# A fused attention, feed-forward and expert kernel: startup steps, the last output weights' tile, one PSUM bank and the tile of the results are rearranged

## The chip, the cores and the metric

The kernel runs on one core of a Trainium2 chip. The metric is the device time of one execution in microseconds (us). Before the change it was 966.34 us, the median of three runs (966.10, 966.34 and 966.62).

## The reference

Three stages work on 3072 tokens of 512 features; all inputs and outputs are float32.

```python
# 1. attention: 4 x 8 heads, 768 positions, head size 64; each chunk of 32 queries sees
#    8 memory keys, 16 keys to the left, its own 32 and 8 to the right (64 in all)
scores = scale * np.matmul(q_c, k_full.transpose(0, 1, 3, 2))
a = np.exp(scores - np.max(scores, axis=-1, keepdims=True))
a = a / (np.sum(a, axis=-1, keepdims=True) + 1e-09)
out[:, :, c_start:c_end] = np.matmul(a, v_full)
# 2. feed-forward, 512 -> 2048 -> 512
r = np.maximum(x @ w_in, 0.0)
x = (r * r) @ w_out
# 3. one of 8 experts per token (the largest gate logit), 512 -> 1024 -> 512
h = np.maximum(x[mask] @ w1[e], 0.0)
out[mask] = gate_w[mask, None] * eom[mask, e, None] * (h @ w2[e])
```

## The kernel before

The tokens are cut into 12 blocks of 256. A `Duo` is the attention of one block, in two units of 128 tokens (`u0`, `u1`). Its steps have names that the profile's rows carry: `scores_mm` multiplies queries with keys on TensorE (tile pss, L161), `scores_max` and `scores_sub` take the row maximum off on VectorE (mx L190, e L195), `scores_exp` is the exponential on ScalarE (L211), `norm` sums and inverts the rows (sm L217, rs L221) and from duo 2 on also scales e itself (L223), `transpose_a` turns e on TensorE (psa, L234) and copies it back on ScalarE (L244), `av` multiplies with the values (psx, L259 or, in the first two duos, L161), and `transpose_x` turns the result into the pieces xhi (L299) and xlo (L303). The four big tiles pss, psa, psx and pst of all duos follow each other in one PSUM buffer, `ps_a`.

A `Block` is the feed-forward of 256 tokens. Products are made of two pieces per operand, hi and lo: `mm1` is 12 products into ph (L410; for two blocks at once L389), `relu` makes r, g, gh on ScalarE (L421, L429, L433) and gl on VectorE (L435), `mm2` is six products into py (L446 to L448). The weights w_in and w_out come as eight tiles each, i0, o0, i1, ... o7, and each is turned into its pieces by five steps: exponent on ScalarE (L327), shift (L332) and two ORs (L339, L343) on VectorE, hi on ScalarE (L352), lo on VectorE (L357). `wo` and `wi` in the rows are these pieces, `ws_o` and `ws_i` the tiles under conversion.

The gate follows block by block (`gate_transpose`, `gate_logits`, `gate_choose`, `gate_rank`). `gate_rank` counts each token's place in its expert's list with two small products into psr (L528, L529), in a buffer of `ps_h`, a ring of two banks that the ph tiles use too. Then come eight experts' `Pair`s of 256 gathered tokens, and single slots of 128. A pair's tiles end in p (ph0p to ph7p are pair products of the first layer, L734; gl0p L745). `Pair.scale` writes the weighted result to o (L698), from where GpSimd scatters it (L704).

The order is written out by hand at the start (L1014 to L1117) and by a table from position n = 4 on: `todo[n]` holds the steps that are issued at position n of the sequence of first-layer products, sorted by `turn`. `bits` gives the position of each weight tile's ORs (its hi and lo follow one position later), `plan_duo` those of a duo's steps. An engine takes its instructions in the order in which they are issued. At the start `keep_busy(n)` issues n dummy products of `ones` (spin, L1011), each 512 columns wide; `hold` (a small GpSimd copy into the tile that a load will fill) delays a load until a given value exists.

Of the kernel before, what the change touches and what calls it, by code (L numbers as in the profile page):

```python
# [8 lines left out]
F32 = mybir.dt.float32  # L9
# [8 lines left out]
P = 128  # L18
NT = 3072
D = 512  # L20
# [4 lines left out]
NB = NT // BLK  # L25
TPB = BLK // P
# [30 lines left out]
def chunk_attention_relu2_moe_top1_kernel(ctx: ExitStack, tc, qk, vv, qt, kv, w_in, w_out, wg, wexp, consts, out):  # L57
    nc = tc.nc
# [5 lines left out]
    ap_ = ctx.enter_context(tc.tile_pool(name="ap", bufs=2))  # L64
# [257 lines left out]
    def split_w_exp(kind, g, halves=None):  # L322
        t = raw[kind, g]
        if (kind, g) not in converted:
            converted[kind, g] = tp.tile([P, 1024], F32, tag="ws", name=f"ws_{kind}{g}", bufs=2)
        for s in slices(halves):
            nc.scalar.activation(converted[kind, g][:, s], t[:, s, 1].bitcast(F32), ACTF.Abs, scale=2.0 ** -111)  # L327

    def split_w_shift(kind, g, halves=None):
        for s in slices(halves):  # L330
            li = converted[kind, g][:, s].bitcast(I32)
            nc.vector.tensor_scalar(li, li, 3, None, op0=ALU.logical_shift_left)  # L332

    def split_w_or(kind, g, halves=None, steps=(0, 1)):
        t = raw[kind, g]
        for s in slices(halves):
            li = converted[kind, g][:, s].bitcast(I32)
            if 0 in steps:
                nc.vector.scalar_tensor_tensor(  # L339
                    li, t[:, s, 0], 29, li, op0=ALU.logical_shift_right, op1=ALU.bitwise_or  # L340
                )
            if 1 in steps:
                nc.vector.scalar_tensor_tensor(  # L343
                    li, t[:, s, 1], -0x80000000, li, op0=ALU.bitwise_and, op1=ALU.bitwise_or
                )

    def split_w_hi(kind, g, halves=None):
        if (kind, g) not in wh:
            w = wpool.tile([P, 2, 1024], F32R, tag=f"{kind}{g}", name=f"w{kind}{g}")
            wh[kind, g], wl[kind, g] = w[:, 0], w[:, 1]  # L350
        for s in slices(halves):
            nc.scalar.copy(wh[kind, g][:, s], converted[kind, g][:, s])  # L352

    def split_w_lo(kind, g, halves=None):
        for s in slices(halves):
            h, lf = wh[kind, g][:, s], converted[kind, g][:, s]
            nc.vector.tensor_tensor(wl[kind, g][:, s], lf, h.bitcast(F32), op=ALU.subtract)  # L357
# [11 lines left out]
    class Block:  # L369
# [152 lines left out]

        def gate_rank(self):
            b = self.b
            ps = ps_h.tile([P, D], F32, tag="h", name=f"psr{b}")
            n = TPB * NE
            ohf = self.oh.rearrange("p t e -> p (t e)")
            nc.tensor.matmul(ps[:, 0:n], lhsT=before, rhs=ohf, start=True, stop=True)  # L528
            nc.tensor.matmul(ps[:, n : 2 * n], lhsT=ones, rhs=ohf, start=True, stop=True)  # L529
            pb = rp.tile([P, TPB, NE], F32, tag="pb", name=f"pb{b}")  # L530
            pos = rp.tile([P, TPB], F32, tag="pos", name=f"pos{b}")
            idx = rp.tile([P, TPB], I32, tag="idx", name=f"idx{b}", bufs=2)
            for t in range(TPB):
                nc.vector.tensor_tensor(pb[:, t], ps[:, t * NE : (t + 1) * NE], base[:, 0:NE], op=ALU.add)
                nc.vector.tensor_tensor(base[:, 0:NE], base[:, 0:NE], ps[:, n + t * NE : n + (t + 1) * NE], op=ALU.add)
            nc.vector.tensor_tensor(pb, pb, self.oh, op=ALU.mult)
            nc.vector.tensor_reduce(out=pos, in_=pb, axis=AX.X, op=ALU.add)
            nc.vector.tensor_copy(idx, pos)  # L538
            for t in range(TPB):
                nc.gpsimd.indirect_dma_start(  # L540
                    out=listd,
                    out_offset=bass.IndirectOffsetOnAxis(ap=idx[:, t : t + 1].bitcast(U32), axis=0),
                    in_=ent[:, b * TPB + t, :],
                    in_offset=None,
                )
# [89 lines left out]
    class Entry:  # L635
# [50 lines left out]
        def scale(self, t, po, shared=False):  # L686
            c = self.col + t
            if self.tiles == 1:
                o = qp.tile([P, D], F32, tag="q", name=f"o{c}")
            else:  # L690
                if t == 0:
                    self.o = ap_.tile([P, TPB, D], F32, tag="e", name=f"o{c}", bufs=1)
                o = self.o[:, t]
            self.y[t] = o
            weight = slots[:, c, 1:2].bitcast(F32)
            on_act = 0 if self.tiles > 1 else D // 2 if shared else D
            if on_act < D:
                nc.vector.tensor_scalar(o[:, on_act:], po[:, on_act:], weight, None, op0=ALU.mult)  # L698
            if on_act > 0:
                nc.scalar.activation(o[:, :on_act], po[:, :on_act], ACTF.Copy, scale=weight)  # L700
# [160 lines left out]
    def plan_duo(b, s, m, t, v, last=None):  # L861
        d = duos[b]
        plan(s, d.scores)
        plan(m, d.norm)
        plan(t, d.transpose_a)
        plan(v, d.av)
        if last is None:
            plan(v, d.transpose_x_copy)
        else:
            ahead[last] = d.transpose_x_copy  # L870
        if b + 1 < NB:
            plan(s + 1, duos[b + 1].load_q, 0)
            plan(s + 1, duos[b + 1].load_q, 1)
        if 2 < b < NB - 1:
            plan(v + 1, duos[b + 1].load_kv, 1)
        if b < NB - 2:
            plan(v + 2, duos[b + 2].load_kv, 0)
# [5 lines left out]
        plan(c, bl.gate_choose)  # L883
        plan(r, bl.gate_rank)

    bits = dict(zip(range(3, 16), (2, 4, 6, 8, 10, 12, 14, 15, 17, 18, 20, 21, 23)))
    for m, n in bits.items():
        if m > 4:
            plan(bits[m - 1], split_w_exp, *tiles[m])
# [13 lines left out]
    plan(bits[15] + 1, duos[3].load_kv, 1)  # L903
    plan(23, lambda: prepare())
    n = at[2, 0]
    plan_duo(2, n - 7, n - 6, n - 4, n - 3)
    plan_duo(3, n + 1, n + 2, n + 5, n + 6)
    plan_gate(0, n + 7, n + 9, n + 15, n + 18)
    plan_duo(4, n + 11, n + 13, n + 15, n + 17)
# [2 lines left out]
    for g in range(2, GROUPED - 1):  # L912
        n = at[2 * g, 0]
# [74 lines left out]
    with tc.manual_schedule():  # L988
# [6 lines left out]
        def hold(tile_, until):  # L995
            nc.gpsimd.tensor_copy(tile_[0:1, 0:1], until)
# [9 lines left out]

        spin = ps_h.tile([P, 4, P], F32, tag="h", name="spin")

        def keep_busy(n):
            for _ in range(n):  # L1010
                nc.tensor.matmul(spin, lhsT=ones, rhs=ones.unsqueeze(1).to_broadcast([P, 4, P]), start=True, stop=True)  # L1011

        u0, u1, other = (0,), (1,), (ps_y, "y")
        keep_busy(12)  # L1014
        d0.scores_mm(u0)
        keep_busy(4)
        d0.scores_max(u0)
        i0t = load_w(*i0, issue=False)
        hold(i0t[:, 1024:].bitcast(F32), d0.mx[u0][0:1, 0, 0:1])
# [7 lines left out]
        d0.scores_exp(u0)  # L1027
        d0.transpose_a_mm(u0)
        d0.transpose_a_copy(u0)
        keep_busy(3)  # L1030
        d0.scores_max(u1)
        d0.scores_sub(u1)
        d0.scores_exp(u1)
# [1 line left out]
        d0.norm(u0)  # L1035
        d0.av_mm(u0)
        d0.av_scale(u0)
        split_w_shift(*i0, a)
        split_w_or(*i0, a, steps=(0,))
        d0.transpose_a_mm(u1, *other)  # L1040
# [3 lines left out]
        split_w_exp(*i0, b)  # L1044
        keep_busy(2)
        d0.av_mm(u1, *other)
        d0.transpose_x_lo(u0)
        d0.norm(u1)
        i1t = load_w(*i1, issue=False)
        hold(i1t.bitcast(F32), d0.r[u1][0:1, 0, 0:1])  # L1050
        load_w(*i1)
        nc.sync.dma_start(cst[:, P:], consts[:, P:])
        d0.av_scale(u1)
        keep_busy(5)
        split_w_or(*i0, a, steps=(1,))
        d0.transpose_x_mm(u1, *other)
        split_w_shift(*i0, b)
        split_w_hi(*i0, a)
        d0.transpose_x_hi(u1)
        split_w_or(*i0, b, steps=(0,))  # L1060
        split_w_lo(*i0, a)
        d0.transpose_x_lo(u1)
        split_w_or(*i0, b, steps=(1,))
        d1.scores_mm()
        keep_busy(2)
        b0.mm1_products(0)
        split_w_hi(*i0, b)
        load_w(*o1)
        d1.scores_max()
        split_w_lo(*i0, b)  # L1070
        split_w_exp(*o0)
        keep_busy(3)
        d1.scores_sub()
        b0.relu(0)
        b0.mm1_products(1)
        d1.scores_exp()
        split_w_shift(*o0)
        split_w_or(*o0, steps=(0,))
        keep_busy(3)
        d1.transpose_a_mm()  # L1080
        d1.norm()
        split_w_or(*o0, steps=(1,))
        load_w(*i2)
        b0.relu(1)
        d1.transpose_a_copy()
        keep_busy(3)
        d1.av_mm()
        split_w_exp(*i1)
        split_w_hi(*o0)
        d1.av_scale()  # L1090
        split_w_lo(*o0)
        keep_busy(5)
        d1.transpose_x_mm()
        split_w_shift(*i1)
        d1.transpose_x_hi()
        b0.mm2(0)
        d1.transpose_x_lo()
        split_w_exp(*o1)
        b0.mm2(1)
        split_w_or(*i1)  # L1100
        load_w(*o2)
        b1.mm1_products(0)
        split_w_shift(*o1)
        b1.relu(0)
        split_w_hi(*i1)
        b1.mm1_products(1)
        split_w_lo(*i1)
        b1.mm2(0)
        split_w_or(*o1)
        b1.relu(1)  # L1110
        split_w_exp(*i2)
        split_w_hi(*o1)
        split_w_shift(*i2)
# [167 lines left out]
```

## Time and profile before

| what | value |
|---|---|
| median of three runs | 966.34 us |
| the profiled execution | 967.47 us, of it the span 965.5 us |
| TensorE (PE) busy | 945.5 us, 98% of the span |
| VectorE (DVE) busy | 600.1 us, 62% |
| ScalarE (ACT) busy | 453.2 us, 47% |
| GpSimd (POOL) busy | 98.6 us, 10% |
| granted TensorE clock, mean | 0.997 of full |

PE is the engine that carries the program, so the time is its busy time plus its waits plus what a lower clock costs it. A row of the timeline gives start, duration, engine, line, operation, written and read tiles, and in square brackets how long the engine was idle before it and whom it waited for. "issue" means that it waited for nothing that the profile shows.

### The profile page before, as it was taken

The numbers are of one execution on the slowest core, as the hardware profiler recorded it, in microseconds if no ns is written. First come the engines' busy times: TensorE is split into PE (matmuls) and PEld (weight loads), VectorE is DVE, ScalarE is ACT, GpSimd is POOL, SyncE is SP. The second block draws the span as 40 slices with busy tenths as digits, with TensorE's granted clock in tenths as the row PEclk, the third lists the DMA queues.
The fourth block names the chain that finished last, engine by engine and source line by source line (L and its number), as shares of the span: only waits on it lengthen the run. The fifth ranks groups of instructions, "written<-read, shape, count | busy, mean of one in ns | idle before, by whom it ended". The sixth has DMA issues, their size and how long they took to land. (4 is left out here: it accounts for less than half of the span.)

```text
span 965.5 us, 19444 instructions
## 1 busy us (share of the span) xinstructions
PE 945.5 (98%) x7862; PEld 792.1 (82%) x7862; DVE 600.1 (62%) x1125; ACT 453.2 (47%) x816; POOL 98.6 (10%) x93
## 2 busy tenths in 40 slices
PE   7999899999999999999999999999999999999996
PEld 4787789888888888888888888888899999888885
DVE  6999553554445345534553454668776666799995
ACT  4787433323233233332322333545455445688885
POOL 0100000000000000000000011012232212122221
PEclk9999999999999999999999999999999999999999
DMA  9466423223120212021100106360876656553631
GB/s 367 155 223 234 150 87 99 76 24 103 39 76 23 76 67 76 23 75 54 51 1 2 45 1 246 134 240 15 325 309 221 236 209 244 191 188 131 218 124 42
DMA packets 30991, 125.51 MB, mean 130 GB/s; under 512 B 8559, under 2 KB 9071, under 8 KB 21554
## 3 DMA queue, kind: packets, MB, share of 16 engines
q1 hardware_dynamic: 25650, 110.30, 31.9%
q0 software_dynamic: 5248, 13.92, 4.1%
q8 instruction: 64, 1.05, 0.5%
q14 instruction: 29, 0.24, 0.1%
HBM read 138.65 MB, written 13.61 MB: 158 GB/s over the span
## 5 line engine op out<-in xcount | busy, mean ns | idle before, releaser
L389 PE MATMUL ph<-xhi,wi 128*128 128x512 f32 x688 | 212.6, 390 | 0.3 <-DVE wi L357 0.3
L421 ACT ACTIVATE r<-ph 128x256 f32<-128x256 f32 x192 | 72.2, 376 | 234.5 <-PE ph L389 199.0
L431 DVE TENSOR_TENSOR g<-r 128x256 f32<-128x256 f32 x160 | 67.4, 422 | 183.6 <-ACT r L421 183.6
L446 PE MATMUL py<-wo,gh 128*128 128x512 f32 x384 | 156.4, 407 | 0.8 <-ACT gh L433 0.8
L389 PEld LDWEIGHTS ph<-xhi,wi 128*128 128x128 f32 x688 | 129.1, 188 | 28.4 <-DVE wi L357 1.2
L448 PE MATMUL py<-wo,gl 128*128 128x512 f32 x384 | 150.4, 392 | 0.0
L447 PE MATMUL py<-wo,gh 128*128 128x512 f32 x384 | 150.4, 392 | 0.0
L389 PE MATMUL ph<-xlo,wi 128*128 128x512 f32 x344 | 133.9, 389 | 0.0
L683 DVE TENSOR_TENSOR x<-raw,x 128x1024 fp32r<-128x1024 f32 x88 | 103.2, 1222 | 7.0 <-ACT x L682 5.4
L435 DVE TENSOR_TENSOR gl<-g,gh 128x256 fp32r<-128x256 f32 x192 | 81.4, 425 | 31.0 <-ACT gh L433 9.8
L683 DVE TENSOR_TENSOR p<-raw,p 128x1024 fp32r<-128x1024 f32 x64 | 78.2, 1222 | 23.1 <-ACT p L682 23.1
L682 ACT CAST x<-raw 128x1024 fp32r<-128x1024 f32 x88 | 87.3, 1056 | 0.0
L446 PEld LDWEIGHTS py<-wo,gh 128*128 128x128 f32 x384 | 72.3, 188 | 17.3 <-issue 2.0
L448 PEld LDWEIGHTS py<-wo,gl 128*128 128x128 f32 x384 | 72.2, 188 | 16.2 <-DVE gl L435 0.6
L433 ACT ACTIVATE gh<-r 128x256 fp32r<-128x256 f32 x192 | 79.9, 416 | 10.4 <-PE py L447 2.3
L447 PEld LDWEIGHTS py<-wo,gh 128*128 128x128 f32 x384 | 72.4, 189 | 12.5
L540 POOL DMA_INDIRECT listd<-ent,idx x24 | 25.5, 1061 | 555.1 <-DVE idx L538 336.9
L389 PEld LDWEIGHTS ph<-xlo,wi 128*128 128x128 f32 x344 | 64.6, 188 | 13.5
L682 ACT CAST p<-raw 128x1024 fp32r<-128x1024 f32 x64 | 66.6, 1041 | 1.2 <-DMA raw<-in_wexp 1.2
L834 PE MATMUL po<-x,ht 128*128 128x512 f32 x264 | 65.4, 397 | 0.6 <-DVE ht L824 0.6
L704 POOL DMA_INDIRECT out<-o,slots x27 | 37.5, 1390 | 208.6 <-ACT o L700 91.4
L834 PEld LDWEIGHTS po<-x,ht 128*128 128x128 f32 x264 | 48.1, 188 | 10.2 <-DVE ht L824 1.0
(229 smaller groups left out, 1455.7 us busy)
## 6 DMA issues: line engine op xcount, KB each, us to landing
raw<-in_wexp SPq DMA_DIRECT2D x82, 1024.0 KB
kv<-in_kv SPq DMA_DIRECT2D x19, 880.0 KB
raw_o<-in_w_out SPq DMA_DIRECT2D x8, 1024.0 KB
raw_i<-in_w_in SPq DMA_DIRECT2D x7, 1024.0 KB
ydram<-y SPq DMA_DIRECT2D x24, 256.0 KB
q<-in_qt SPq DMA_DIRECT2D x20, 256.0 KB
qk<-in_qk SPq DMA_DIRECT2D x4, 624.0 KB
v<-in_vv SPq DMA_DIRECT2D x2, 1024.0 KB
```

The lines of the kernel that those rows point to most:

```text
L389: nc.tensor.matmul(ph.rearrange("p (s c) -> p s c", s=2), lhsT=w_in_part(w, f, k), rhs=x[:, s, k, :], start=(n == 0), stop=(n == 11),)
L421: nc.scalar.activation(self.r, self.ph, ACTF.Relu, scale=WSCALE)
L431: nc.vector.tensor_tensor(g, r, r, op=ALU.mult)
L433: nc.scalar.activation(gh, r, ACTF.Square)
L435: nc.vector.tensor_tensor(gl, g, gh.bitcast(F32), op=ALU.subtract)
L446: nc.tensor.matmul(self.y[t], lhsT=gh[:, s], rhs=w_out_part(wh, f), start=(f == 0), stop=False)
L447: nc.tensor.matmul(self.y[t], lhsT=gh[:, s], rhs=w_out_part(wl, f), start=False, stop=False)
L448: nc.tensor.matmul(self.y[t], lhsT=gl[:, s], rhs=w_out_part(wh, f), start=False, stop=(f == NF - 1))
L682: nc.scalar.copy(w[:, 0], t)
L683: nc.vector.tensor_tensor(w[:, 1], t, w[:, 0].bitcast(F32), op=ALU.subtract)
L704: nc.gpsimd.indirect_dma_start(out=out, out_offset=bass.IndirectOffsetOnAxis(ap=slots[:, c, 0:1].bitcast(U32), axis=0), in_=self.y[t], in_ ...
L834: nc.tensor.matmul(self.po, lhsT=self.ht[:, part, f, :], rhs=w[:, wp, j * D : j * D + D], start=(f == 0 and part == 0 and wp == 0), stop=( ...
```

## The change

It has five parts. (1) For the last two blocks `gate_rank` takes its bank from `ps_a` instead of the ring `ps_h`. (2) `Pair.scale` takes a tile for each half from the ring t2 (four buffers) instead of both halves in the one buffer of tag e. (3) Tile 15, the last output weights o7, has its ORs at position 26 instead of 23, hi and lo at 27 instead of 24, and with them duo 3's load of keys at 27 instead of 24. (4) Duo 2's `norm` is issued at position 25, with its scores, instead of 26. (5) The start is written in another order: duo 1's scores, maximum and the rest come ahead of the ORs of the second half of i0, block 1's first-layer products ahead of block 0's second layer, and the dummy products are other ones: 36 of 128 columns instead of 12 of 512, 6 of 256 instead of 4 of 512, 10 of 128 instead of 3 of 512, and later ones partly left out.

```diff
         def gate_rank(self):
             b = self.b
-            ps = ps_h.tile([P, D], F32, tag="h", name=f"psr{b}")
+            if b < NB - 2:
+                ps = ps_h.tile([P, D], F32, tag="h", name=f"psr{b}")
+            else:
+                ps = ps_a.tile([P, TPB, D], F32, tag="a", name=f"psr{b}")[:, 0]
...
             else:
-                if t == 0:
-                    self.o = ap_.tile([P, TPB, D], F32, tag="e", name=f"o{c}", bufs=1)
-                o = self.o[:, t]
+                o = tp.tile([P, D], F32, tag="t2", name=f"o{c}")
...
-    bits = dict(zip(range(3, 16), (2, 4, 6, 8, 10, 12, 14, 15, 17, 18, 20, 21, 23)))
+    bits = dict(zip(range(3, 16), (2, 4, 6, 8, 10, 12, 14, 15, 17, 18, 20, 21, 26)))
...
-    plan_duo(2, n - 7, n - 6, n - 4, n - 3)
+    plan_duo(2, n - 7, n - 7, n - 4, n - 3)
...
-        keep_busy(12)
+        keep_busy(36, 1)
         d0.scores_mm(u0)
-        keep_busy(4)
+        keep_busy(6, 2)
...
-        split_w_or(*i0, b, steps=(0,))
         split_w_lo(*i0, a)
         d0.transpose_x_lo(u1)
-        split_w_or(*i0, b, steps=(1,))
+        keep_busy(3)
         d1.scores_mm()
-        keep_busy(2)
         b0.mm1_products(0)
-        split_w_hi(*i0, b)
+        d1.scores_max()
+        d1.scores_sub()
+        split_w_or(*i0, b)
         load_w(*o1)
-        d1.scores_max()
-        split_w_lo(*i0, b)
+        keep_busy(3)
+        d1.scores_exp()
         split_w_exp(*o0)
...
         d1.transpose_a_mm()
         d1.norm()
+        d1.transpose_a_copy()
+        split_w_hi(*i0, b)
+        b0.relu_r(0)
+        split_w_shift(*o0)
+        split_w_lo(*i0, b)
...
+        b1.mm1_products(1)
         b0.mm2(0)
```

The first place is VectorE around the two ORs of o7 and duo 2's maximum; ws_o7 is the tile under conversion, wo7 its lo piece, gl0_12 to gl1_13 are lo pieces of activations of block 0 and 1, and mx2, e2, sm2 and rs2 belong to duo 2. On VectorE before:

```order
L339 SCALAR_TENSOR_TENSOR ws_o7_1142<-raw_o7_1087,ws_o7_1142 128x1024
L343 SCALAR_TENSOR_TENSOR ws_o7_1142<-raw_o7_1087,ws_o7_1142 128x1024
L435 TENSOR_TENSOR gl0_12_1231<-g0_12_1227,gh0_12_1229 128x256
L357 TENSOR_TENSOR wo7_1233<-ws_o7_1142,wo7_1233 128x1024
L435 TENSOR_TENSOR gl1_12_1250<-g1_12_1246,gh1_12_1248 128x256
L190 TENSOR_REDUCE mx2_0_1317<-pss2_0_1252 128x16
L195 TENSOR_TENSOR e2_1319<-pss2_0_1252,mx2_0_1317 128x2x8x64
L207 MEMSET e2_1319 32x8x8
L435 TENSOR_TENSOR gl0_13_1348<-g0_13_1344,gh0_13_1346 128x256
L217 TENSOR_REDUCE sm2_0_1350<-e2_1319 128x16
L218 TENSOR_SCALAR sm2_0_1350<-sm2_0_1350 128x16
L221 RECIPROCAL rs2_0_1353<-sm2_0_1350 128x16
```

On VectorE after the change the same place reads:

```order
L435 TENSOR_TENSOR gl0_12_1253<-g0_12_1249,gh0_12_1251 128x256
L435 TENSOR_TENSOR gl1_12_1267<-g1_12_1263,gh1_12_1265 128x256
L190 TENSOR_REDUCE mx2_0_1334<-pss2_0_1269 128x16
L195 TENSOR_TENSOR e2_1336<-pss2_0_1269,mx2_0_1334 128x2x8x64
L207 MEMSET e2_1336 32x8x8
L217 TENSOR_REDUCE sm2_0_1340<-e2_1336 128x16
L218 TENSOR_SCALAR sm2_0_1340<-sm2_0_1340 128x16
L221 RECIPROCAL rs2_0_1343<-sm2_0_1340 128x16
L223 TENSOR_TENSOR e2_1336<-e2_1336,rs2_0_1343 128x1024
L435 TENSOR_TENSOR gl0_13_1371<-g0_13_1367,gh0_13_1369 128x256
L339 SCALAR_TENSOR_TENSOR ws_o7_1166<-raw_o7_1111,ws_o7_1166 128x1024
L343 SCALAR_TENSOR_TENSOR ws_o7_1166<-raw_o7_1111,ws_o7_1166 128x1024
```

The two ORs stand behind duo 2's last scaling of e (L223) instead of ahead of its maximum, the lo piece wo7 is later still, and the sum (L217) no longer stands behind gl0_13.

The second place is ScalarE from duo 2's exponential to the copy of the turned e. On ScalarE before, from o7's hi piece on:

```order
L352 CAST wo7_1233<-ws_o7_1142 128x1024
L421 ACTIVATE r1_12_1244<-ph0_12_1212 128x256
L429 ACTIVATE g1_12_1246<-r1_12_1244 128x256
L433 ACTIVATE gh1_12_1248<-r1_12_1244 128x256
L211 ACTIVATE e2_1319<-e2_1319 128x1024
L421 ACTIVATE r0_13_1342<-ph0_13_1329 128x256
```

On ScalarE after the change, from the exponential on:

```order
L211 ACTIVATE e2_1336<-e2_1336 128x1024
L421 ACTIVATE r0_13_1365<-ph0_13_1352 128x256
L429 ACTIVATE g0_13_1367<-r0_13_1365 128x256
L433 ACTIVATE gh0_13_1369<-r0_13_1365 128x256
L421 ACTIVATE r1_13_1385<-ph0_13_1352 128x256
L429 ACTIVATE g1_13_1387<-r1_13_1385 128x256
L433 ACTIVATE gh1_13_1389<-r1_13_1385 128x256
L352 CAST wo7_1393<-ws_o7_1166 128x1024
L421 ACTIVATE r0_14_1417<-ph0_14_1404 128x256
L429 ACTIVATE g0_14_1419<-r0_14_1417 128x256
L433 ACTIVATE gh0_14_1421<-r0_14_1417 128x256
L244 COPY e2_1336<-psa2_0_1425 128x1024
```

The hi piece of o7 has gone from ahead of the exponential to a place ahead of three activations of block 0 and of the copy (L244).

The third place is VectorE at the start, around duo 1's maximum; ws_i0 and wi0 are the second half of the first weights (one wi0 and one OR are of the first half), xlo is duo 0's. On VectorE before:

```order
L343 SCALAR_TENSOR_TENSOR ws_i0_236<-raw_i0_123,ws_i0_236 128x512
L332 TENSOR_SCALAR ws_i0_236<-ws_i0_236 128x512
L339 SCALAR_TENSOR_TENSOR ws_i0_236<-raw_i0_123,ws_i0_236 128x512
L357 TENSOR_TENSOR wi0_351<-ws_i0_236,wi0_351 128x512
L303 TENSOR_TENSOR xlo_110<-pst0_1_345,xhi_109 128x4x128
L343 SCALAR_TENSOR_TENSOR ws_i0_236<-raw_i0_123,ws_i0_236 128x512
L190 TENSOR_REDUCE mx1_0_441<-pss1_0_358 128x16
L357 TENSOR_TENSOR wi0_351<-ws_i0_236,wi0_351 128x512
L195 TENSOR_TENSOR e1_449<-pss1_0_358,mx1_0_441 128x2x8x64
```

On VectorE after the change:

```order
L332 TENSOR_SCALAR ws_i0_269<-ws_i0_269 128x512
L357 TENSOR_TENSOR wi0_382<-ws_i0_269,wi0_382 128x512
L303 TENSOR_TENSOR xlo_110<-pst0_1_376,xhi_109 128x4x128
L190 TENSOR_REDUCE mx1_0_468<-pss1_0_390 128x16
L195 TENSOR_TENSOR e1_470<-pss1_0_390,mx1_0_468 128x2x8x64
L339 SCALAR_TENSOR_TENSOR ws_i0_269<-raw_i0_123,ws_i0_269 128x512
L343 SCALAR_TENSOR_TENSOR ws_i0_269<-raw_i0_123,ws_i0_269 128x512
L217 TENSOR_REDUCE sm1_0_491<-e1_470 128x16
L218 TENSOR_SCALAR sm1_0_491<-sm1_0_491 128x16
L221 RECIPROCAL rs1_0_494<-sm1_0_491 128x16
L332 TENSOR_SCALAR ws_o0_480<-ws_o0_480 128x1024
L357 TENSOR_TENSOR wi0_382<-ws_i0_269,wi0_382 128x512
```

The maximum stood behind both ORs of the second half and now stands ahead of them, and that half's lo piece (the last row) comes behind duo 1's sum instead of right behind the maximum.

## Rows read from the trace of the kernel before

**Rows 1.** Page: busy time of the engines, with shares and counts of instructions

```profile
PE 945.5 (98%) x7862; PEld 792.1 (82%) x7862; DVE 600.1 (62%) x1125; ACT 453.2 (47%) x816; POOL 98.6 (10%) x93
```

**Rows 2.** Waits of PE: sum, times, longest, in us

```profile
PE psa L234 <- DVE e L223: 3.2, 1, 3.2
PE pss L161 <- issue: 2.1, 1, 2.1
PE ph2p L734 <- DVE gl2p L745: 1.8, 1, 1.8
...
PE ph1p L734 <- DVE gl0p L745: 0.8, 1, 0.8
```

**Rows 3.** Windows: length, busy us (instructions) by engine, granted clock, DMA

```profile
core 0: us, PE busy (x) PEld busy (x) DVE busy (x) ACT busy (x) POOL busy (x), PEclk, DMA share, GB/s
...
13.00:24.00 11.00, 8.10 (x229) 6.13 (x228) 9.39 (x16) 5.38 (x10) 0.18 (x1) 1.00 1.02 422
...
42.00:108.00 66.00, 65.20 (x406) 52.71 (x405) 60.86 (x73) 49.23 (x93) 0.00 (x0) 1.00 0.67 235
...
112.00:117.00 5.00, 4.96 (x86) 4.06 (x90) 0.99 (x3) 2.13 (x4) 0.00 (x0) 0.66 0.01 3
...
650.00:692.00 42.00, 39.35 (x252) 35.00 (x251) 32.28 (x87) 19.48 (x30) 11.25 (x9) 1.00 0.36 134
```

**Rows 4.** Timeline of PE at the start

```profile
16.34 0.76 PE L161 MATMUL pss<-qk 64*32 64x64 f32 x52
19.17 1.00 PE L161 MATMUL pss<-qk 64*32 64x64 f32 x76 [2.07 <-issue]
```

**Rows 5.** Timeline of DVE at the start

```profile
20.21 1.23 DVE L190 TENSOR_REDUCE mx<-pss 128x16 f32<-128x1024 f32 x1 [0.99 <-PE pss L161]
...
37.41 1.23 DVE L357 TENSOR_TENSOR wi<-ws_i,wi 128x1024 fp32r<-128x1024 f32 x1 [0.51 <-ACT wi L352]
```

**Rows 6.** Timeline of DVE around o7 and duo 2's maximum

```profile
98.65 1.22 DVE L339 SCALAR_TENSOR_TENSOR ws_o<-raw_o,ws_o 128x1024 int32<-128x1024 int32 x1
99.90 1.23 DVE L343 SCALAR_TENSOR_TENSOR ws_o<-raw_o,ws_o 128x1024 int32<-128x1024 int32 x1
...
102.25 1.23 DVE L357 TENSOR_TENSOR wo<-ws_o,wo 128x1024 fp32r<-128x1024 f32 x1 [0.78 <-ACT wo L352]
...
103.72 1.22 DVE L190 TENSOR_REDUCE mx<-pss 128x16 f32<-128x1024 f32 x1
...
108.93 1.21 DVE L217 TENSOR_REDUCE sm<-e 128x16 f32<-128x1024 f32 x1
...
110.67 1.23 DVE L223 TENSOR_TENSOR e<-e,rs 128x1024 f32<-128x1024 f32 x1
```

**Rows 7.** Timeline of ACT in the same stretch

```profile
98.80 0.40 ACT L433 ACTIVATE gh<-r 128x256 fp32r<-128x256 f32 x1
101.16 1.05 ACT L352 CAST wo<-ws_o 128x1024 fp32r<-128x1024 f32 x1 [1.96 <-DVE ws_o L343]
...
106.47 1.06 ACT L211 ACTIVATE e<-e 128x1024 f32<-128x1024 f32 x1 [3.22 <-PE py L448]
...
113.14 1.01 ACT L244 COPY e<-psa 128x1024 f32<-128x1024 f32 x1 [2.54 <-PE psa L234]
```

**Rows 8.** Timeline of PE around duo 2's psa and psx

```profile
112.04 1.06 PE L234 MATMUL psa<-cst,e 128*128 128x128 f32 x8 [3.22 <-DVE e L223]
112.86 0.48 PE L446 MATMUL py<-wo,gh 128*128 128x512 f32 x1
113.18 0.43 PE L447 MATMUL py<-wo,gh 128*128 128x512 f32 x1
...
115.25 0.32 PE L259 MATMUL psx<-e,v 64*64 64x32 f32 x2
...
```

**Rows 9.** Timeline of PE at the next to last rank

```profile
654.92 0.51 PE L734 MATMUL ph1p<-xhi,p 128*128 128x256 f32 x2 [0.82 <-DVE gl0p L745]
```

**Rows 10.** Timeline of DVE at the first pair's results

```profile
690.08 1.41 DVE L698 TENSOR_SCALAR o<-po,slots 128x512 f32<-128x512 f32 x2 [1.31 <-DMA out<-o,slots]
```

More of the change, by code (lines that the diff above doesn't have):

```diff
@@ L1007, in chunk_attention_relu2_moe_top1_kernel, with keep_busy @@
         spin = ps_h.tile([P, 4, P], F32, tag="h", name="spin")
-        def keep_busy(n):
+        def keep_busy(n, k=4):
             for _ in range(n):
-                nc.tensor.matmul(spin, lhsT=ones, rhs=ones.unsqueeze(1).to_broadcast([P, 4, P]), start=True, stop=True)
+                nc.tensor.matmul(
+                    spin[:, :k], lhsT=ones, rhs=ones.unsqueeze(1).to_broadcast([P, k, P]), start=True, stop=True
+                )
         u0, u1, other = (0,), (1,), (ps_y, "y")
-        keep_busy(12)
+        keep_busy(36, 1)
         d0.scores_mm(u0)
-        keep_busy(4)
+        keep_busy(6, 2)
         d0.scores_max(u0)
@@ L1029, in chunk_attention_relu2_moe_top1_kernel @@
         d0.transpose_a_copy(u0)
-        keep_busy(3)
+        keep_busy(10, 1)
         d0.scores_max(u1)
@@ L1037, in chunk_attention_relu2_moe_top1_kernel @@
         d0.av_scale(u0)
+        d0.norm(u1)
         split_w_shift(*i0, a)
@@ L1046, in chunk_attention_relu2_moe_top1_kernel @@
         d0.av_mm(u1, *other)
-        d0.transpose_x_lo(u0)
-        d0.norm(u1)
+        d0.av_scale(u1)
         i1t = load_w(*i1, issue=False)
-        hold(i1t.bitcast(F32), d0.r[u1][0:1, 0, 0:1])
+        hold(i1t.bitcast(F32), d0.x[0:1, 4, 0, 0:1])
         load_w(*i1)
         nc.sync.dma_start(cst[:, P:], consts[:, P:])
-        d0.av_scale(u1)
-        keep_busy(5)
         split_w_or(*i0, a, steps=(1,))
+        d0.transpose_x_lo(u0)
+        keep_busy(3)
         d0.transpose_x_mm(u1, *other)
+        d0.transpose_x_hi(u1)
@@ L1057, in chunk_attention_relu2_moe_top1_kernel @@
+        split_w_hi(*i0, a)
         split_w_shift(*i0, b)
-        split_w_hi(*i0, a)
-        d0.transpose_x_hi(u1)
-        split_w_or(*i0, b, steps=(0,))
         split_w_lo(*i0, a)
         d0.transpose_x_lo(u1)
-        split_w_or(*i0, b, steps=(1,))
+        keep_busy(3)
         d1.scores_mm()
-        keep_busy(2)
         b0.mm1_products(0)
-        split_w_hi(*i0, b)
+        d1.scores_max()
+        d1.scores_sub()
+        split_w_or(*i0, b)
         load_w(*o1)
-        d1.scores_max()
@@ L1070, in chunk_attention_relu2_moe_top1_kernel @@
-        split_w_lo(*i0, b)
+        keep_busy(3)
+        d1.scores_exp()
         split_w_exp(*o0)
[L1072 to L1079, printed above, removed]
         d1.transpose_a_mm()
         d1.norm()
+        d1.transpose_a_copy()
[3 more added lines that the diff above has]
+        split_w_lo(*i0, b)
+        keep_busy(3)
@@ L1082, in chunk_attention_relu2_moe_top1_kernel @@
+        d1.av_mm()
+        d1.av_scale()
+        b0.mm1_products(1)
+        split_w_or(*o0, steps=(0,))
+        b0.relu_g(0)
+        d1.transpose_x_mm()
+        d1.transpose_x_hi()
         split_w_or(*o0, steps=(1,))
         load_w(*i2)
+        d1.transpose_x_lo()
+        split_w_hi(*o0)
         b0.relu(1)
-        d1.transpose_a_copy()
-        keep_busy(3)
-        d1.av_mm()
+        b1.mm1_products(0)
         split_w_exp(*i1)
-        split_w_hi(*o0)
-        d1.av_scale()
         split_w_lo(*o0)
-        keep_busy(5)
@@ L1093, in chunk_attention_relu2_moe_top1_kernel @@
-        d1.transpose_x_mm()
         split_w_shift(*i1)
-        d1.transpose_x_hi()
+        b1.relu(0)
+        b1.mm1_products(1)
         b0.mm2(0)
-        d1.transpose_x_lo()
-        split_w_exp(*o1)
-        b0.mm2(1)
         split_w_or(*i1)
         load_w(*o2)
-        b1.mm1_products(0)
+        b0.mm2(1)
+        split_w_exp(*o1)
+        b1.relu(1)
+        split_w_hi(*i1)
         split_w_shift(*o1)
-        b1.relu(0)
-        split_w_hi(*i1)
-        b1.mm1_products(1)
         split_w_lo(*i1)
@@ L1109, in chunk_attention_relu2_moe_top1_kernel @@
         split_w_or(*o1)
-        b1.relu(1)
         split_w_exp(*i2)
```

## The prediction

> **What bounds the kernel now.** I read the page first: PE is busy for 945.5 us, 98% of the span [rows 1], so an edit counts only if it moves PE. The second view is the list of PE's waits. It is short: 3.2 us for duo 2's scaled e, 2.1 us of "issue" inside a score product, 1.8 and 0.8 us at the first pair's products [rows 2]. Third come the windows, which show what a wait costs behind it: the granted clock is 1.00 everywhere I list but in 112 to 117, right behind the 3.22 us wait, where it is 0.66 [rows 3, 8]. Fourth, the timelines of DVE, ACT and PE around each wait, to see who was late. The change touches exactly these places, so it is priced place by place.
>
> **The start.** Here DVE sets the pace: 9.39 of 11.00 us busy from 13 to 24 [rows 3]. PE stops for 2.07 us in the middle of duo 1's scores, with nothing that it waits for, between 16.34 + 0.76 = 17.10 and 19.17 [rows 4]; DVE's maximum waits 0.99 us for it [rows 5]. The change takes no work off DVE up to the lo piece of the second weights (37.41, [rows 5]); it reorders. Two ORs of the second half and their lo piece go behind the maximum, and each is as large as half a row of 1.22 us [rows 6], so DVE reaches the maximum some 1.2 us sooner.
>
> If the scores came without a stop, at 17.10 plus the 1.00 us of their rest, DVE would wait for nothing: −1.0 us. If the stop ends at the same 19.17, DVE only waits 1.2 us longer, since the moved work runs later: +1.2. A further stop of the same size in the next product that DVE or ACT needs (psa of duo 1) makes it more, and the lo piece now stands behind ACT's hi piece, which ACT issues behind duo 1's exponential; the nearest row for such a wait is 0.51 us [rows 5]. I take +2.1 (one stop as in [rows 4]) as the upper end and, between −1.0 and +2.1, the middle: +0.5. The dummy products themselves stand where PE waits anyway; 36, 6 and 10 of them instead of 12, 4 and 3 are 33 more, with a weight load each, and fewer columns, and I count their time at nothing. The cover is PE's wait for the first maximum and exponentials; without it they would cost what their columns cost.
>
> The stop in [rows 4] has no releaser in the trace, and the DMA engines are full just then (share 1.02 from 13 to 24, [rows 3]). The Trainium skill (Runtime: NRT & Kernel Launch, "Instruction fetch mechanics") says that instructions come in blocks of 256 by a DMA queue of the engine's own, and that crossing a block is mostly hidden. A stop of 2.07 us agrees with the fetch but not with "hidden". By that section the 33 added products, 66 instructions, would move the block edges by a quarter of a block, and the stop to another place; by [rows 4] alone it would stay where it is.
>
> **Duo 2's place.** Before, DVE does from 98.65 on two ORs (2.5 us by their starts), a wait of 0.78 us for ACT, the lo piece (1.23 us) and two short gl, and starts the maximum at 103.72 [rows 6]. The ORs, the wait and the lo piece go: 4.5 us. But the second gl needs three activations on ACT, which no longer stand behind the hi piece: 98.80 + 0.40 = 99.2 [rows 7], plus 1.1 (three of 0.40 that overlap a little), plus 0.4 for the gl: the maximum starts at 100.7 instead of 103.72. From maximum to exponential it is 106.47 − 103.72 = 2.75 us [rows 6, 7], so the exponential runs from 103.45 to 104.5. The sum follows at once, since gl0_13 now stands behind it, and sum to scaled e takes 110.67 + 1.23 − 108.93 = 2.97 us [rows 6]: e is ready at 107.5. PE is done with its work ahead at 112.04 − 3.22 = 108.82 [rows 8]. The wait of 3.22 us goes.
>
> With it goes the low clock. Of the stretch behind the wait, psa and six products take 112.04 to 115.25 = 3.21 us [rows 8], at starts 0.32 to 0.43 us apart; at full clock they would take half, so 1.6 are lost there, and psx begins at half clock too. By the mean, 0.34 × 5.00 = 1.7 us are lost in 112 to 117 [rows 3]. I take 2.0. So the place costs 3.2 + 2.0 = 5.2 us.
>
> What is late next: the copy of the turned e on ACT, which psx waits for. On DVE the two ORs now follow the scaled e: 107.5 + 0.4 (gl0_13) + 2.5 = 110.4. ACT's hi piece of o7 waits for them, and the first-come order puts it ahead of three activations and of the copy: 110.4 + 1.05 (hi) + 1.1 + 1.01 (copy) [rows 7] = 113.6. PE would want to start psx at 108.82 + 1.6 = 110.4. That is a new wait of 3.2 us in place of the old one, no shorter than it. What is gained is then only the clock, if it holds: a wait of 2.07 us [rows 4] left it at 1.00 [rows 3], one of 3.22 did not. Here PE has worked 1.6 us between, and if the start makes PE later by half a us while DVE, which has 66.00 − 60.86 = 5.1 us to spare from 42 to 108 [rows 3], catches up, the new wait is 2.7. I choose that it holds: −5.2 + 3.2 = −2.0. If it falls again, 0; if the new wait doesn't come at all, −5.2. Duo 3's load of keys, three positions later, is hidden: nothing is moved from 108 on for some us, and it is needed ten positions later.
>
> **The pairs.** With the next to last rank in `ps_a`, ph1p has its bank at once and the 0.82 us [rows 9] go; the buffer's next writer is the last rank, some 4 us later, so nobody waits. But 35 us on, DVE's two results stand idle for 1.31 us until the scatter that reads the old tile is done, take 1.41 together, and gl2p is behind them [rows 10], for which PE waits 1.84 us [rows 2]. The scatters hang on GpSimd's queue, which PE doesn't lead, so the 0.82 are waited for again here. The ring of four gives the first result a free tile; the second one takes the place of a tile whose scatter is out. So one result, 0.7 us, comes ahead of the wait. Net −0.7; ends 0 and −(0.82 + 1.84) = −2.7.
>
> **Sum.** The profiled execution is 967.47 us, 1.13 over the median of the runs. 967.47 + 0.5 − 2.0 − 0.7 = 965.3; less 1.13 it is 964.1.
>
> **Rivals.** *The clock falls at duo 2 all the same.* The new wait is as long as the old one, which speaks for it; the 1.6 us of work between speak against. Then that place gives 0: 966.1. *The new wait is short.* The ORs could find DVE earlier than I count, or PE later, and then ACT's copy is in time: −5.2 there, 960.9. Against it: my walk has no slack of 3 us. *The stop of the start comes twice more* (the slower side). It sits in duo 1's scores, where the DMA engines are full; in the changed order psa and psx of duo 1 stand ahead of every first-layer product of block 1, and each stop of 2.07 us in them is paid in full because ACT and DVE have nothing else that PE could use. Two of them: 2 × 2.07 = 4.1 instead of +0.5, so 964.1 + 3.6 = 967.7, slower by 1.4; it decides from the second stop on. Speaking against it: the DMA share falls after 24 us, and before the change psa at that time stopped for nothing of its own. *The ring changes nothing* (both results still wait for the scatter): 964.8, inside the forecast's own range.
>
> **How the numbers follow.** Forecast 0.37 (964.1, own range 962.8 to 965.4), clock falls 0.27 (966.1), short wait 0.20 (960.9), two more stops 0.16 (967.7). The bounds of the start (−1.0, +2.1) and of the pairs (0, −2.7) widen each by about 1.5. The range of 8 in 10 is 960.4 to 967.9. About 0.2%, 1.9 us, is what a measurement of this kernel tells from no change: faster means under 964.4. That is 0.6 of the forecast, nearly all of the short wait and a little of the clock's case: 0.45. Slower, over 968.3, needs two stops and more: 0.13. The same: 0.42.
>
> **What would show it.** In PE's list of waits, psa's 3.2 us must go and a wait of psx for ACT's copy of about 3 us must stand there; a window over it with the clock at 1.00 makes the forecast, at about 0.66 the first rival. DVE's maximum of duo 2 must come about 3 us sooner against PE's first-layer products. In the first 40 us the "issue" stops count: one of 2 us is the forecast, three the third rival. ph1p must not wait at 655, and gl2p's wait must stay above 1 us. The forecast is wrong if PE enters the steady part more than 2 us later or 1 us earlier than before.

## The result: slower by 0.8%, lost in the first 45 us

The changed kernel takes 973.62 us (median of 4 runs, 972.35 to 975.88) against 966.37 us; the ratio is 1.0078, with a 95% interval of 1.0065 to 1.0091. The forecast was 964.1 us. The profiled execution took 972.35 us, 4.88 more than that of before. Of the ten runs of after_o1_held, below, one took 4095.78 us, and its ratio leaves this run out.

The list of PE's waits of the changed kernel (engine, waiting line, releaser: sum, times, longest, in us) answers to [rows 2]:

```profile
PE psx L161 <- issue: 4.3, 2, 2.7
PE psx L259 <- ACT e L244: 2.1, 1, 2.1
PE psa L234 <- ACT e L211: 2.1, 2, 1.4
PE ph L410 <- ACT xhi L299: 1.1, 1, 1.1
...
PE ph2p L735 <- DVE gl2p L746: 1.0, 1, 1.0
...
PE ph L410 <- DVE xlo L303: 0.8, 1, 0.8
...
PE psa L234 <- issue: 0.4, 1, 0.4
```

The 3.2 us for duo 2's scaled e and the 0.8 us of ph1p are gone, and gl2p's wait is shorter. In their place stand 4.3 us of "issue" in psx at the start, 2.1 us of duo 2's psx for the copy on ScalarE, and 1.1 and 0.8 us of ph for duo 1's xhi and xlo. The windows of the changed kernel (length, busy us and instructions by engine, granted clock, DMA share, GB/s) answer to [rows 3]:

```profile
13.00:24.00 11.00, 9.35 (x225) 6.03 (x223) 9.36 (x16) 3.94 (x7) 0.57 (x1) 0.84 0.89 361
24.00:34.00 10.00, 6.45 (x152) 5.36 (x153) 6.08 (x10) 3.54 (x6) 1.47 (x6) 0.83 0.31 108
34.00:42.00 8.00, 6.14 (x35) 5.64 (x34) 5.53 (x8) 6.12 (x11) 0.00 (x0) 0.79 0.37 131
42.00:108.00 66.00, 64.97 (x403) 52.14 (x402) 61.60 (x75) 50.99 (x95) 0.00 (x0) 1.00 0.62 219
108.00:112.00 4.00, 4.00 (x19) 3.34 (x18) 2.82 (x4) 0.99 (x2) 0.00 (x0) 1.00 0.88 293
112.00:117.00 5.00, 5.00 (x26) 4.17 (x26) 4.75 (x7) 2.07 (x7) 0.00 (x0) 1.00 0.03 8
117.00:130.00 13.00, 10.90 (x162) 8.93 (x161) 4.36 (x6) 6.09 (x13) 0.00 (x0) 0.87 0.41 140
...
650.00:692.00 42.00, 41.93 (x288) 37.90 (x287) 32.28 (x85) 21.52 (x34) 12.09 (x10) 1.00 0.31 108
```

The clock's column is the new thing. It stands at 0.84, 0.83 and 0.79 from 13 to 42 us, where it was 1.00, and at 0.87 behind duo 2's wait. By these shares the first three windows lost 0.16 × 11 + 0.17 × 10 + 0.21 × 8 = 5.1 us, part of it under dummy products and waits. Where that began, the PE timeline of the start shows (start, us, engine, line, tiles, count, and the wait ahead):

```profile
9.90 0.64 PE L161 MATMUL psx<-v,spare_o 64*32 64x64 f32 x38
12.16 0.43 PE L161 MATMUL psx<-v,spare_o 64*32 64x64 f32 x26 [1.62 <-issue]
...
18.54 1.61 PE L161 MATMUL pss<-qk 64*32 64x64 f32 x128
...
20.70 0.40 PE L410 MATMUL ph<-xhi,wi 128*128 128x256 f32 x2
...
24.83 0.81 PE L234 MATMUL psa<-cst,e 128*128 128x128 f32 x6 [0.38 <-issue]
...
26.75 1.40 PE L161 MATMUL psx<-v,spare_o 64*32 64x64 f32 x119 [0.45 <-ACT spare_o L244]
30.85 0.44 PE L161 MATMUL psx<-v,spare_o 64*32 64x64 f32 x9 [2.70 <-issue]
...
32.03 0.63 PE L410 MATMUL ph<-xhi,wi 128*128 128x256 f32 x2
32.45 0.41 PE L410 MATMUL ph<-xlo,wi 128*128 128x256 f32 x1
...
45.66 0.39 PE L389 MATMUL ph<-xhi,wi 128*128 128x512 f32 x1
```

PE stops without a releaser in the first duo's psx (1.62 us, after 38 of 64 products), shortly in duo 1's psa (0.38) and 9 products before the end of duo 1's psx (2.70). Duo 1's scores, where the stop was [rows 4], run through. From the third product of psa (24.83) to the stop in psx are 6 + 3 + 119 = 128 products; with a weight load each these are 256 instructions, and as many lie between the two stops of before (12.26 and 19.17 us). The place where such a block of 256 ends is called an edge below. From the 2.70 us stop on, two xhi products and one xlo product take 0.64 us (32.03 to 32.67, where the next one starts), and they took 0.35 in the same program before it (20.70 to 21.05). The products from 31 to 34 us run at this half pace and, behind the waits for xhi (1.10) and xlo (0.76), those from 37.7 to 40.6; between them the clock was full again:

```profile
34.00:36.00 2.00, 0.97 (x9) 0.74 (x7) 1.19 (x2) 0.99 (x2) 0.00 (x0) 1.00 0.00 0
...
38.00:40.00 2.00, 2.00 (x11) 2.00 (x11) 1.96 (x3) 1.20 (x3) 0.00 (x0) 0.50 0.64 270
```

The last row of the PE timeline is the first product of block 2 for two blocks at once, from where on the order on PE is the old one. It comes at 45.66 and came at 37.99 before: **the start costs 7.7 us**. From 9.9 us to this product PE's "issue" stops grew from 2.28 to 4.70 us, its other waits from 1.8 to 4.0 us, and its busy time from 24.1 to 27.1 us, though there were nine dummy products fewer.

The DVE rows around duo 2's maximum and the ACT and PE rows to psx answer to [rows 6 to 8]:

```profile
108.27 1.22 DVE L190 TENSOR_REDUCE mx<-pss 128x16 f32<-128x1024 f32 x1
...
113.86 1.23 DVE L223 TENSOR_TENSOR e<-e,rs 128x1024 f32<-128x1024 f32 x1
...
115.34 1.22 DVE L339 SCALAR_TENSOR_TENSOR ws_o<-raw_o,ws_o 128x1024 int32<-128x1024 int32 x1
116.59 1.22 DVE L343 SCALAR_TENSOR_TENSOR ws_o<-raw_o,ws_o 128x1024 int32<-128x1024 int32 x1
```

```profile
117.85 1.05 ACT L352 CAST wo<-ws_o 128x1024 fp32r<-128x1024 f32 x1 [3.72 <-DVE ws_o L343]
...
119.84 0.99 ACT L244 COPY e<-psa 128x1024 f32<-128x1024 f32 x1
```

```profile
116.35 1.04 PE L234 MATMUL psa<-cst,e 128*128 128x128 f32 x8
...
118.38 0.40 PE L448 MATMUL py<-wo,gl 128*128 128x512 f32 x1
120.88 0.25 PE L259 MATMUL psx<-e,v 64*64 64x32 f32 x2 [2.10 <-ACT e L244]
...
123.63 0.63 PE L447 MATMUL py<-wo,gh 128*128 128x512 f32 x1
```

Against PE's block 2 products the maximum comes 3.1 us sooner than before (108.27 − 103.72 − 7.67 = −3.1). PE reaches psa without a wait, does psa and the six products by 118.8 and waits 2.10 us for the copy, which stands behind the hi piece of o7 (117.85) on ScalarE, as that stands behind the OR of 116.59. Behind it the second layer's products start 0.43 us apart instead of 0.23: the clock fell again. At a row further on (block 2's second products, 126.30 before, 132.80 now) the lag is 6.5 us, so duo 2's place gave back 7.7 − 6.5 = 1.2 us. At the end the lag is 4.9: from the pairs on 1.6 us came back.

The first pair's results, to be read against [rows 10]:

```profile
694.94 1.39 DVE L699 TENSOR_SCALAR o<-po,slots 128x512 f32<-128x512 f32 x2
```

The wait of 1.31 us for the scatter is gone from the row.

### The profile page after: what moved, and what is told of

Its sections match the earlier page's. It is cut to its first block, busy times and chain, and to the rows that moved or that the text cites. A ratio compares the mean times of both kernels' runs of the same rounds, so it can differ in the third digit from the quotient of the medians.

```text
span 970.4 us, 19491 instructions
## 1 busy us (share of the span) xinstructions
PE 948.5 (98%) x7886; PEld 798.4 (82%) x7886; DVE 600.8 (62%) x1125; ACT 453.0 (47%) x816; POOL 95.9 (10%) x93
```

## The experiments

Each was timed beside the kernel before on the same chip. "rest" below is the kernel before with parts 1 to 4 and the old start.

**The start alone (start_only).** The kernel before with the whole new start (the last part of the diff above) and nothing else.

> The kernel before with the new start alone. Theory 'start': all of the loss is made before position 4, so this is slower than the kernel before by the 7.7 us that the first-layer product of block 2 came late, 973 to 975 us, with an issue stop of about 2.7 us in duo 1's psx and a granted clock near 0.8 from 24 to 42 us. Rival 'sum': the later parts cost time too, and the start alone loses less than 5 us.

973.76 us against 965.54, ratio 1.0081 (1.0066 to 1.0096). The stop in duo 1's psx is there with 2.70 us, and the clock is 0.80 from 24 to 34 us and 0.50 from 34 to 42. The start is the whole loss.

**The rest alone (rest_only).**

> The kernel before with parts 1 to 4, without the new start. Theory 'start': the rest gains what the two traces show behind the start, 1.2 us at duo 2 and 1.6 us from the pairs on, so 963.2 to 964.5 us. Rival 'sum': 966 us or slower, since duo 2's new wait falls on an earlier PE.

962.25 us against 965.54, ratio 0.9963 (0.9949 to 0.9976): the other four parts gain 3.3 us, about 1 us more than I had expected. That is more than in the changed kernel, though its psx waits 2.1 us as well; ph1p and ph2p wait for nothing.

**o1 held back (after_o1_held).** In the changed kernel:

```diff
-        load_w(*o1)
         d1.scores_exp()
...
         d1.av_scale()
+        o1t = load_w(*o1, issue=False)
+        hold(o1t.bitcast(F32), d1.x[0:1, 0, 0, 0:1])
+        load_w(*o1)
```

> The changed kernel with the 1 MB load of o1 held back until duo 1's attention result exists, so that no load is on the DMA engines between 24 and 30 us. Theory 'load in the way': the next block of instructions waits behind this load, and without it the 2.7 us issue stop in duo 1's psx goes or falls under 0.7 us, the clock stays at 1.00 behind it and the time is 966 to 969 us. Rival 'edge alone': a block of instructions takes about 6 us to come whatever else is moved, the stop stays at 2 us or more and the time over 971 us. A later o1 may cost up to 1 us in either case.

967.35 us against 965.54, ratio 1.0017 (1.0008 to 1.0027): about 5.4 of the 7.3 us are gone by moving one load. The queue of the loads in the changed kernel, and in this one:

```profile
24.20 0.33 SPq L316 DMA_DIRECT2D raw_o<-in_w_out  x1
```

```profile
30.99 0.33 SPq L316 DMA_DIRECT2D raw_o<-in_w_out  x1
```

In the changed kernel o1's load is issued at 24.20, 0.6 us ahead of the block edge in psa, and the next edge waits 2.70 us. Without the load, in the PE timeline of this kernel, the same edge of psx waits 0.23:

```profile
11.95 0.43 PE L161 MATMUL psx<-v,spare_o 64*32 64x64 f32 x26 [1.41 <-issue]
...
24.63 0.81 PE L234 MATMUL psa<-cst,e 128*128 128x128 f32 x6 [0.43 <-issue]
...
28.18 0.32 PE L161 MATMUL psx<-v,spare_o 64*32 64x64 f32 x9 [0.23 <-issue]
```

This tells "load in the way" from "edge alone": the edge stands where it stood, and the stop is a tenth as long. What PE waited for stands in the DMA view (packets, MB, share), which has a queue of kind "instruction": 64 packets of 16 KB in the whole execution. These are the page's row, the changed kernel's rows from 26 to 28 and from 28 to 30 us, and this kernel's row from 24 to 26 us:

```profile
q8 instruction: 64, 1.05, 0.5%
```

```profile
q1 hardware_dynamic: 98, 0.80, 96.3%
```

```profile
...
q8 instruction: 1, 0.02, 3.0%
```

```profile
q8 instruction: 1, 0.02, 3.0%
```

In the changed kernel the packet starts at 28.7 us, when o1's load (queue q1) is through, 3.9 us behind the edge in psa; it ends at 29.6, and PE goes on at 30.85. With o1 held it starts at 25.9, 1.3 us behind the same edge, ends at 26.8, and PE goes on at 28.18. In all runs, each "issue" stop of PE up to 40 us, 23 of them, ends 1.2 to 1.5 us behind the end of such a packet. So the load delays the packet, and the packet PE; what fills the last 1.2 us isn't shown.

The clock from 24 to 34 us is 1.00 instead of 0.83. From 34 to 42 us it is 0.79 as in the changed kernel: the half pace there comes behind waits of 1.10 and 1.21 us for duo 1's xhi and xlo, and not behind the stop. The remaining loss against rest, 5 us, isn't taken apart here; the stop of 1.4 us at 11, these waits and the low clock are in it.

**Old dummies in the new order (after_wide).** `keep_busy(12)`, `(4)` and `(3)` instead of `(36, 1)`, `(6, 2)` and `(10, 1)`.

> The changed kernel with the first dummy products of the kernel before (12, 4 and 3 of 512 columns instead of 36 of 128, 6 of 256 and 10 of 128): 33 products fewer ahead of the same work. Theory 'block edges': the stops move 33 products on, out of duo 1's psx and into block 1's or block 0's products behind it; the stop is then at another place but of some length still, and the time within 968 to 973 us. Rival 'dummies': the low clock comes from too few dummy columns, it stays at 1.00 here, and the time is under 968 us with the stop still in psx. Rival 'order': neither matters, and the time stays at 972 us or more with the same low clock.

965.09 us against 965.54, ratio 1.0002 (0.9987 to 1.0016), less than the 968 to 973 that I had expected. The stops stand in duo 0's pst and duo 1's scores, as in the kernel before; the PE timeline shows them:

```profile
12.29 0.27 PE L234 MATMUL pst<-cst,spare_i 128*128 128x128 f32 x1 [0.27 <-issue]
...
18.55 1.01 PE L161 MATMUL pss<-qk 64*32 64x64 f32 x77 [2.01 <-issue]
```

No psx at the start has one, and the clock is 1.00 up to 112 us. Block 2's first product comes at 39.1; in five runs with the whole old start it came at 37.2 to 38.5. In the medians the new order costs 2.8 us against rest. The stop moved by the number of the products taken out; its place is a matter of counting.

**Half the narrow dummies (after_few).** 18, 3 and 5 instead of 36, 6 and 10.

> The changed kernel with half of its first narrow dummy products (18, 3 and 5 instead of 36, 6 and 10): 26 products and half of the dummy columns fewer. Theory 'block edges': the edges come 26 products later in the same work, so the one at the end of duo 1's psx leaves it, the stop there falls under 1 us or stands elsewhere, the clock from 34 to 42 us is above 0.9 and the time is 964 to 969 us although there are fewer dummy columns. Rival 'dummy columns': the clock hangs on the columns of the dummies; with half of them it is lower than in the changed kernel in the first 42 us, and the time 973 us or more.

966.66 us against 965.15, ratio 1.0013 (0.9999 to 1.0027). The stop of 2.7 us is gone from psx; one of 1.1 us stands in the following pst. With half the dummy columns the clock from 34 to 42 us is 0.86, not below the 0.79 of the changed kernel, but also not above 0.9 as I had set. That the clock hangs on the dummies' columns alone is ruled out; that they have no part in it isn't.

**New dummies in the old order (before_narrow).**

> The kernel before with only the new first dummy products (36 of 128, 6 of 256, 10 of 128 columns instead of 12, 4 and 3 of 512). Theory 'block edges and the load behind them': the edges come 33 products earlier, so the stop in duo 1's scores comes a few products earlier and stays about 2 us, no stop is in psx, the clock from 24 to 42 us is 1.00 and the time is within 2 us of the kernel before. Rival 'narrow dummies': they let the clock fall in the old order too, the clock from 24 to 42 us is under 0.9 and the time 3 us or more above.

968.76 us against 965.57, ratio 1.0033 (1.0023 to 1.0044). The clock from 24 to 42 us is 1.00 and no stop is in duo 1's psx, as the block edges want it. But it is slower by 3.2 us, more than I allowed: the stop went from duo 1's scores, where I had expected it, to the first duo's psx (1.5 us), with a clock of 0.84 from 13 to 24 us behind it; block 2's first product comes 1.0 us later, and a part of the rest shows as a lower clock behind duo 2's wait (0.74 from 108 to 117 and 0.92 from 117 to 130, where it was 0.81 and 1.00). Why the fall at duo 2 lasts longer there isn't settled.

**The bank and the ring by themselves (bank_only, ring_only).** Parts 1 and 2, one run each.

> The kernel before with the last two ranks' bank from the other ring alone. By the prediction: ph1p's wait of 0.8 us goes, and gl2p's wait grows by as much, to about 2.6 us, since the scatter of the first result comes when it came. Rival 'scatter comes earlier': the rank's reads on VectorE come earlier and with them the lists and the scatter, gl2p's wait does not grow, and 0.8 us or more are gained.

> The kernel before with the ring for the results alone. By the prediction one result of 0.7 us comes ahead of the wait for the scatter: gl2p's wait falls from 1.8 to about 1.1 us, ph1p's 0.8 us stays. Rival: both results get a free tile and the wait goes entirely, 1.8 us.

They took 964.61 and 965.95 us against 965.15; one run each doesn't tell such times apart. With the bank alone ph1p's wait goes and gl2p's is 0.6 us; with the ring alone ph1p's stays and gl2p's goes. From the POOL timeline, the first list scatter and the second result scatter, before and with the bank:

```profile
656.31 1.73 POOL L540 DMA_INDIRECT listd<-ent,idx  x1 [6.63 <-DVE idx L538]
...
681.70 1.98 POOL L704 DMA_INDIRECT out<-o,slots  x1 [4.83 <-DMA slots<-listd]
```

```profile
655.57 1.73 POOL L543 DMA_INDIRECT listd<-ent,idx  x1 [6.64 <-DVE idx L541]
...
678.77 0.99 POOL L707 DMA_INDIRECT out<-o,slots  x1 [4.45 <-DVE p L686]
```

The next to last rank on PE comes 0.73 us earlier there (651.67 instead of 652.40; the start was that much shorter), the last rank 1.6 (654.85 instead of 656.46), since ph1p ahead of it no longer waits, and the second scatter 2.9. So the scatter comes earlier with the last rank, and the prediction's "waited for again" is wrong: gl2p's wait grew in no run. How much the rank moves the scatter isn't shown. With the ring alone, where both ranks stand as before, the chain from the next to last rank to the second scatter is shorter by 1.3 us too (2.2 with the bank). And gl2p's wait of 1.8 us before is 0.9 in start_only and 0.7 in before_narrow, which have neither part, so the 0.6 with the bank need not come from it.

**The hi piece behind the copy (rest_hi_later).** In rest:

```diff
             plan(n, split_w_or, *tiles[m])
-            plan(n + 1, split_w_hi, *tiles[m])
-            plan(n + 1, split_w_lo, *tiles[m])
+            if m < 15:
+                plan(n + 1, split_w_hi, *tiles[m])
+                plan(n + 1, split_w_lo, *tiles[m])
...
     plan_duo(2, n - 7, n - 7, n - 4, n - 3)
+    plan(n - 4, lambda: split_w_hi(*tiles[15]))
+    plan(n - 4, lambda: split_w_lo(*tiles[15]))
```

> Parts 1 to 4 without the new start, and o7's hi and lo pieces issued behind the copy of duo 2's turned e instead of ahead of it. Theory 'copy behind hi': psx waits 2.1 us for the copy only because ScalarE makes the hi piece first; here that wait falls under 0.7 us, the clock stays at 1.00 from 108 to 130 us, and the time is 3 to 4 us under that of parts 1 to 4 alone, 958 to 960 us. Rival 'wait moves on': the hi piece is then late for the second layer of block 0, which waits as long, and the time stays at 962 us or more.

959.04 us against 965.15, ratio 0.9932 (0.9918 to 0.9945). **It beats both kernels.** Its waits of PE hold no psx L259 at all; the longest and that of the second layer are those below, and the windows behind duo 2 (same columns as above) are at full clock with PE busy throughout:

```profile
PE pst L234 <- DVE spare_i L274: 1.8, 3, 1.1
...
PE py L446 <- ACT gh L433: 0.8, 1, 0.8
```

```profile
108.00:117.00 9.00, 9.00 (x164) 7.57 (x163) 5.10 (x7) 5.04 (x10) 0.00 (x0) 1.00 0.59 201
117.00:130.00 13.00, 13.00 (x198) 11.57 (x197) 8.06 (x14) 5.40 (x13) 0.00 (x0) 1.00 0.16 58
```

The hi piece comes in time for block 0's second layer. Against rest that is 3.2 us, more than the 2.1 us of the wait; the remainder fits the clock, which in rest is 0.57 from 112 to 117 us and 0.90 from 117 to 130.

**And i1 held (best_i1_held).** On top of that, i1's load held until duo 1's maximum.

> Parts 1 to 4 with o7's hi piece behind the copy (959.0 us when measured), and now the load of i1 held until duo 1's maximum instead of the first duo's row sums, so that no load of 1 MB is under way around 17 us. Theory 'load in the way': the issue stop in duo 1's scores falls under 0.3 us, and where it was 0.4 to 2 us long up to that much is gained, 957.5 to 959 us, if the later i1 and o1 cost nothing. Rival: i1 comes too late for the conversion of the second weights, a wait on its pieces of 1 us or more appears before 45 us, and the time is above 959.5 us.

960.60 us against 965.57, ratio 0.9947 (0.9933 to 0.9961): no gain. The stop in the scores is still 1.2 us, with the DMA engines still 0.74 busy from 13 to 24 us with loads issued earlier, and a new one stands where the held loads now are. In the PE timeline:

```profile
18.26 1.00 PE L161 MATMUL pss<-qk 64*32 64x64 f32 x76 [1.23 <-issue]
...
30.89 0.77 PE L234 MATMUL pst<-cst,spare_i 128*128 128x128 f32 x5 [1.30 <-issue]
```

The second stop follows the loads to their new place, which fits "load in the way"; that the first one would go is refuted. No wait on i1's pieces appeared.

## Why the prediction was wrong

**The start** is the step that failed: "+0.5", with "+2.1 (one stop as in [rows 4])" as the upper end. It cost 7.7 us, where "more than 2 us later" was the prediction's own sign of being wrong. Three things in it were wrong. The dummies: "I count their time at nothing". Their time was nothing (the first duo's psx starts at 9.90 us, at 9.86 before), their number was not. 33 products more put the block edges in the first duo's psx and at the end of duo 1's psx, where 1 MB of o1 had just been put on the DMA engines by the same reordering; taking the 33 out or moving the load each takes 5 to 8 us off (after_wide, after_o1_held). The stops come to 4.70 us, 2.4 more than before.

The clock: I priced a stop at its own length. Before, the stop of 2.07 us left the clock at 1.00 [rows 3, 4], and I took this as a rule. It was luck: in ring_only, whose start is the old one, a stop of 1.18 us in the same place was followed by half pace, and the window that has 1.00 in [rows 3] reads

```profile
13.00:24.00 11.00, 8.99 (x227) 6.72 (x205) 9.07 (x15) 4.91 (x10) 0.17 (x1) 0.84 1.02 420
```

In the changed kernel half pace followed on the stops of 1.62 and 2.70 us and on the two waits for duo 1's pieces, and PE's busy time grew by 3.0 us, for which the forecast had no term.

The order: block 1's products now stand ahead of block 0's second layer and wait for duo 1's xhi and xlo (1.10 and 0.76 us), and psa waits 1.43 us for duo 1's exponential. PE's waits of this kind grew by 2.2 us; the forecast had only a row of 0.51 us for such a wait. By themselves the dummies cost 3.2 us (before_narrow) and the order 2.8 (after_wide against rest); together they cost 10.5 (the 7.25 of the changed kernel and the 3.29 that rest gains), so 4.5 us come only where the two meet.

The Trainium skill (Runtime: NRT & Kernel Launch, "Instruction fetch mechanics") has the blocks of 256 instructions and a DMA queue for them: the stop did move when the count changed, 256 instructions lie between two stops of the trace, and the DMA view has the queue, with packets of 16 KB. That crossing a block is mostly hidden, as it says, does not hold here, at 1.62 and 2.70 us.

**The rival of two more stops** had the right mechanism and the right place, psx of duo 1, at 0.16 and 967.7 us. It was mis-sized: it had 4.1 us of stops and nothing else; the stops brought 2.4, the waits for ScalarE's and VectorE's pieces 2.2 and the clock 3.0.

**Duo 2's place** went as worked out up to the sizes: psa's wait went, the wait of psx for the copy came, 2.1 us instead of 3.2. ScalarE's copy ended 4.5 us after psa's start (119.84 + 0.99 − 116.35), forecast 4.8; but psa and the six products took PE 2.4 us at full clock (116.35 to 118.8) and not the 1.6 that I got by halving 3.21. By the same error I charged 0.8 us too much to the low clock of before. "I choose that it holds" was wrong, the clock fell, as the first rival said; −1.2 us instead of −2.0.

**The pairs** gave −1.6 instead of −0.7, −2.7 being the end that I had set. Half of it is ph1p's wait, which went in every run with the bank and wasn't waited for again; the other half is gl2p's, 1.0 us here and 1.8 before, and as it is 0.7 and 0.9 in two runs with the old pairs, this half may be chance.

The sum of the measured terms is +7.7 − 1.2 − 1.6 = +4.9, the difference of the two profiled executions. The medians differ by 7.3: the profiled execution of before lies 1.1 us above its median and that of the changed kernel 1.3 below. Two of the four runs were 974.6 and 975.9 us with mean clocks of 0.986 and 0.987 against 0.992 in the profiled one, which fits a fallen clock that also makes the time vary.

## What to carry to other kernels

A dummy instruction isn't free because it fills a wait: it moves every later instruction against the points where the engine must fetch the next block, so count instructions between the stops in a trace and look which large load is under way where the next stop will fall; the DMA view shows the blocks as packets of a queue of their own. Price a stop of TensorE with the granted clock behind it, and treat a clock that held once as luck, not as a bound. When a conversion is moved off one critical operand, look at what it now stands ahead of on the other engine: moving it one step further, behind the copy, was worth about as much again as the four good parts together (962.3 to 959.0 us, after 965.5).

## What was not expected of the hardware

The wait for a block of instructions depended on the data loads under way: 2.70 us with a 1 MB load issued 0.6 us ahead of the edge before, 0.23 us without it, at the same instruction. The block's packet started 3.9 us behind that edge with the load and 1.3 us without it. In the old start the stop in duo 1's scores came 76 products before their end, but was 0.4, 0.6, 1.2 or 2.1 us long from kernel to kernel, and in rest there was none: there the scores began at 17.19 us instead of 16.34, and the packet, over at 16.6, was in time. And the clock fell to half behind idle stretches of 1.1 to 2.7 us in some runs and held in others: it held behind 2.07 us before and behind 2.01 us in after_wide, and fell behind 1.18 us in ring_only and behind 2.10 us at duo 2 in the changed kernel, there for about 3 us. In start_only's profiled run it stayed at 0.50 from 34 to 42 us, where the changed kernel's came back between.
